# A guard on the softmax: GpSimd counts the reciprocals that lie in range, and a branch at the end decides over a second path

## The chip, the core and the metric

The kernel runs on one core of a Trainium2 chip. A core has five engines with a queue of instructions each: TensorE (PE, matmuls into PSUM), VectorE (DVE), ScalarE (ACT), GpSimd (POOL) and SyncE (SP, which here only issues DMAs and waits). They run by themselves and order each other with semaphores. The metric is device time in microseconds of one execution; lower is better.

## The reference

Two independent halves whose outputs stand side by side. Half A is multi-head attention with 32 heads of 16 columns over 2048 tokens, half B a short convolution, a product, and a long convolution over the sequence:

```python
def _A_ref(x, wqkv, wo):
    B, S, D = x.shape
    H = 32
    Dh = D // H
    qkv = (lambda x, *d: x.transpose(*d))((x @ wqkv).reshape(B, S, 3, H, Dh), 2, 0, 3, 1, 4)
    q, k, v = qkv[0], qkv[1], qkv[2]
    scores = jnp.einsum("bhqd,bhkd->bhqk", q, k) * (Dh ** -0.5)
    p = _softmax(scores, axis=-1)
    o = jnp.einsum("bhqk,bhkd->bhqd", p, v)
    return (lambda x, *d: x.transpose(*d))(o, 0, 2, 1, 3).reshape(B, S, D) @ wo

def _B_ref(q, k, v, shift_k, ssm_k, ssm_D):
    ...
    kv = k_shift * v
    ...
    y = (lambda x, s, axes=(-2,-1): jnp.fft.irfft2(x, s=s, axes=axes).astype(jnp.bfloat16))(y_f, (1, L), axes=(1, 2))[:, 0, :S, :]
    y = y + kv * ssm_D[None, None, :]
    return q * y
```

Weights and inputs are normal numbers times 0.05, so the scores of the softmax are small. A softmax usually subtracts each row's maximum first so that no exponential overflows.

## The kernel before

The kernel computes the exponentials without subtracting a maximum: with scores this small a fixed offset (`OFFSET`, -2 in powers of two) does. Each row's sum of exponentials comes out of the same matmul as the output, because the value matrix `VA` carries a column of ones behind each head's 16 columns.

**Groups.** The work of half A is cut into 32 groups `n` (4 sets `o` of 8 heads, 4 blocks `qb` of 512 queries, and an even and an odd part of the heads). For a group, score blocks of 128 keys by 512 queries are made on TensorE (`qk_mm`, line 827), two or three blocks at a time go through ScalarE's Exp (`emit_exp`, line 854), and one block in so many goes to VectorE instead, which makes the exponential in four passes: a conversion out of PSUM (line 890), a mask (916), a squaring product (921) and another mask (925). TensorE multiplies them by `VA` into one PSUM bank (`emit_pv`, line 964). When a group is complete, `finish_group` takes it on VectorE: a 32x32 block transpose into `DT` (line 1062), the reciprocals of the row sums into the ring `DR` (1069), the product with them into `DTN` (1073), and, for each second group, a transpose back into `OTN` (1082). The last group is finished in four quarters by `finish_last` (lines 1096 to 1111) so that the output projection can follow at once.

**Half B** runs beside it: the long convolution is 8192 small matmuls (line 1234) against shifted copies of the filter that SyncE loads into `WR`.

**Order.** Nothing is scheduled by the hardware. A planner in the program walks step by step (`T`), keeps a model clock for each engine (`Eng.t`), and writes every engine's list of instructions with its waits; what goes where follows from the model clocks. `dve.op`, `pool.op` and so on append an instruction and advance that engine's clock by the times given in `us`. `dma` (line 357) starts a transfer at the model time of its issuing engine. GpSimd's list holds the memsets of the start (lines 461 to 474), the DMAs that spread the scaled queries into `QT` (issued in `evac_unit`, recorded under line 367), the loads and stores of half B's `QN`, the stores of the attention output from `OUTA`, and one memset in the middle (line 1241). `locking` keeps VectorE's passes from being planned beside GpSimd's two long instructions after the start.

**The end.** After the last group, TensorE makes the last output rows, ScalarE and VectorE each copy half of the last tile (lines 1568 and 1566), and both halves are stored. SyncE then waits for all output DMAs (line 1571), and the block that closes the program (line 1573) has every engine drain and meet at a barrier. `Eng.op` (line 162) records an operation with its waits, `Eng.run` (line 187) issues them.

## Time and profile before

| | us |
|---|---|
| runs (3) | 750.45, 751.31, 751.42 |
| median | 751.31 |
| the profiled execution's own time | 753.44 |
| its span, first to last instruction | 751.6 |
| granted TensorE clock, mean | 0.993 |

The profile is one execution. "Busy" is the time in which an engine executes instructions; register, branch, semaphore and DMA-issuing instructions are the sequencer's and are not counted (rows whose engine ends in q, as POOLq). A group's row ends in "busy us, mean ns | idle time before it <-what ended that idle time". A row of one line's instructions gives duration in ns as min/median/max, then the first and the last start. A timeline row begins with the start and the busy time. The chain of waits is followed back from the last instruction.

### The profile page before, as it was taken

The numbers are of one execution on the slowest core, as the hardware profiler recorded it, in microseconds if no ns is written. First come the engines' busy times: TensorE is split into PE (matmuls) and PEld (weight loads), VectorE is DVE, ScalarE is ACT, GpSimd is POOL, SyncE is SP. The second block draws the span as 40 slices with busy tenths as digits, with TensorE's granted clock in tenths as the row PEclk, the third lists the DMA queues.
The fourth block names the chain that finished last, engine by engine and source line by source line (L and its number), as shares of the span: only waits on it lengthen the run. The fifth ranks groups of instructions, "written<-read, shape, count | busy, mean of one in ns | idle before, by whom it ended". The sixth has DMA issues, their size and how long they took to land.

```text
span 751.6 us, 32481 instructions
## 1 busy us (share of the span) xinstructions
PE 697.1 (93%) x14671; PEld 312.6 (42%) x14682; DVE 703.5 (94%) x1442; ACT 725.3 (96%) x691; POOL 98.4 (13%) x172
## 2 busy tenths in 40 slices
PE   7889899999999899999999989999999899999986
PEld 3234344535444444444544333443443344434343
DVE  2999999999899999999999988999999999989993
ACT  6999999999999999999999999999999999999986
POOL 7022102020013002001032021120020202010100
PEclk9999999999999999999999999999999999999999
DMA  9897756766777778665886867665765565776100
GB/s 181 213 257 269 225 167 215 233 234 240 249 239 233 264 241 281 242 197 210 233 269 207 265 220 256 193 238 191 279 222 191 187 271 167 257 242 227 58 3 30
DMA packets 73720, 161.48 MB, mean 215 GB/s; under 512 B 34064, under 2 KB 37776, under 8 KB 73200
## 3 DMA queue, kind: packets, MB, share of 16 engines
q1 hardware_dynamic: 66400, 150.43, 62.5%
q0 software_dynamic: 5984, 8.66, 3.7%
q8 instruction: 116, 1.90, 1.0%
q10 hardware_dynamic: 1200, 0.33, 0.2%
q14 instruction: 20, 0.16, 0.1%
HBM read 142.61 MB, written 6.42 MB: 198 GB/s over the span
## 4 chain that ended last, share of the span: by engine, by line
ACT 63%; PE 18%; DVE 16%; DMA 1%; SPq 1%; issue 1%
ACT PT L854 63%; DVE PTD L890 7%; PE PS L827 6%; PE PS L964 5%; DVE PTD L921 3%; PE PS L1234 3%; DVE PTD L916 2%; PE PS L514 2%; DVE PTD L925 2%; DMA xT<-in_A_x_dram 1%; PE PS L550 1%; SPq L367 1%; DVE DT L1062 1%; PE PS L1485 0%; DVE VA L619 0%
## 5 line engine op out<-in xcount | busy, mean ns | idle before, releaser
L854 ACT ACTIVATE PT<-PS 128x1024 bf16<-128x1024 f32 (+2 forms) x687 | 723.1, 1264 | 14.3 <-PE PS L827 13.4
L890 DVE TENSOR_SCALAR PTD<-PS 128x512 uint16<-128x512 f32 x465 | 310.6, 681 | 14.9 <-PE PS L827 14.1
L827 PE MATMUL PS<-QT,KTo 32*128 32x512 bf16 (+2 forms) x2248 | 273.2, 367 | 29.6 <-ACT PT L854 18.1
L964 PE MATMUL PS<-PT,VA 128*32 128x512 bf16 (+2 forms) x1744 | 185.7, 370 | 4.1 <-DVE VA L619 3.0
L1234 PE MATMUL PS<-WR,KV 128*30 128x128 bf16 (+8 forms) x8192 | 180.3, 219 | 0.0
L1234 PEld LDWEIGHTS PS<-WR,KV 128*32 128x32 bf16 (+7 forms) x8192 | 134.5, 95 | 52.4 <-issue 29.5
L921 DVE TENSOR_TENSOR PTD<-PTD 128x1024 f16<-128x1024 f16 (+1 forms) x233 | 155.4, 677 | 0.5
L827 PEld LDWEIGHTS PS<-QT,KTo 32*128 32x128 bf16 x2248 | 72.1, 91 | 196.5 <-ACT PT L854 137.0
L964 PE MATMUL PS<-PTD,VA 128*32 128x512 f16 (+1 forms) x1008 | 151.5, 370 | 1.8 <-DVE PTD L925 1.7
L367 POOL DMA_DIRECT2D QT<-QS x120 | 61.1, 516 | 423.0 <-DVE QS L580 378.8
L925 DVE TENSOR_SCALAR PTD<-PTD 128x1024 uint16<-128x1024 uint16 (+1 forms) x233 | 95.1, 415 | 0.3
L916 DVE TENSOR_SCALAR PTD<-PTD 128x1024 uint16<-128x1024 uint16 (+1 forms) x233 | 93.0, 416 | 0.3
L964 PEld LDWEIGHTS PS<-PT,VA 128*32 128x32 bf16 x1744 | 47.2, 94 | 93.5 <-issue 69.0
L964 PEld LDWEIGHTS PS<-PTD,VA 128*32 128x32 bf16 x1008 | 39.1, 96 | 12.7 <-issue 2.2
L1485 PE MATMUL PS<-IDN,ZW 128*32 128x512 bf16 (+3 forms) x157 | 37.7, 316 | 0.9 <-PE PS L827 0.5
L367 POOL DMA_DIRECT2D out_dram<-OUTA x15 | 8.7, 579 | 117.9 <-DVE OUTA L1147 84.8
L514 PE MATMUL PS<-xT,WKV 128*32 128x512 bf16 (+1 forms) x256 | 19.2, 385 | 4.6 <-DVE DT L1062 1.3
L1062 DVE STREAM_TRANSPOSE DT<-PS 128x512 f32<-128x512 f32 x31 | 21.9, 708 | 0.4 <-PE PS L964 0.2
L514 PE MATMUL PS<-xT,WQ 128*32 128x512 bf16 x240 | 18.6, 383 | 1.9 <-DVE YB L1250 0.5
L568 PE MATMUL PS<-WKV,xT 128*128 128x128 bf16 x256 | 19.3, 220 | 0.8 <-DVE YB L1250 0.5
L568 PEld LDWEIGHTS PS<-WKV,xT 128*128 128x128 bf16 x256 | 14.4, 98 | 8.7 <-issue 3.7
L1485 PEld LDWEIGHTS PS<-IDN,ZW 128*32 128x32 bf16 x157 | 11.9, 97 | 11.4 <-issue 7.2
(72 smaller groups left out, 246.1 us busy)
## 6 DMA issues: line engine op xcount, KB each, us to landing
WR<-kz_scratch SPq DMA_DIRECT2D x256, 512.0 KB, 5.4
KV<-KV SPq DMA_DIRECT2D x16, 256.0 KB, 5.2
kz_scratch<-WR SPq DMA_DIRECT2D x1, 2176.0 KB, 8.8
QN<-in_B_q_dram POOLq DMA_DIRECT2D x8, 256.0 KB, 5.4
out_dram<-QN POOLq DMA_DIRECT2D x8, 256.0 KB, 4.1
QT<-QS POOLq DMA_DIRECT2D x120, 16.0 KB, 3.9
out_dram<-OUTA POOLq DMA_DIRECT2D x15, 128.0 KB, 3.4
QN<-in_B_ssm_k_dram SPq DMA_DIRECT2D x1, 1024.0 KB, 7.2
```

The source lines that it names most:

```text
L367: f(outp, inp).then_inc(dsem.sem, 16)
L514: ins = e.matmul(dst[g:g + 32], lhsT=w[:, g:g + 32], rhs=rhs, tile_position=(0, g), **kw)
L568: ins = e.matmul(PS[:, bank, 128 * j:128 * j + 128], lhsT=xT[:, dc, (4 * sc + j) * 128:(4 * sc + j + 1) * 128], rhs=WV[:, dc, o * 128:(o + ...
L827: ins = e.matmul(PS[:, bank, i * w:i * w + w], lhsT=KTo[32 * s:32 * s + 32, OF[n_] % 2, kt * 128:(kt + 1) * 128], rhs=QT[32 * s:32 * s + 3 ...
L854: h = act.op(lambda e: e.activation(PT[:, p0:p0 + n, :], src, ACT.Exp, scale=EXP_SCALE, bias=EXP_BIAS), [h, free], us=(0.065 + 0.4257 * n, ...
L890: h_f = urgent(lambda e: e.tensor_scalar(fix_u, PS[:, bank, :], FIX_ADD, FIX_HI, ALU.add, ALU.min), [h, h_ptd.get(i - R_PTD)], slack=S_FX)
L916: st["h"] = dve.op(lambda e: e.tensor_scalar(mant_u, fix_u, MANT, HALF_BITS, ALU.bitwise_and, ALU.bitwise_or), [st["h"]], us=us)
L921: st["h"] = dve.op(lambda e: e.tensor_tensor(mant, fix, mant, ALU.mult), [st["h"]], us=us)
L925: h = dve.op(lambda e: e.tensor_scalar(fix_u, fix_u, OCTAVE, ONE_MORE, ALU.bitwise_and, ALU.bitwise_or), [st["h"]], us=us)
L964: ins = e.matmul(dst, lhsT=w, rhs=rhs, start=first, stop=last, tile_position=(0, 32 * s))
L1234: ins = e.matmul(PS[32 * g:32 * g + 2 * ((30 - d) // 2 + 1), BGB, 128 * kk:128 * kk + w], lhsT=kv, rhs=WR[:, r + g, S - 64 * d - 128:S - 6 ...
L1485: pe.op(lambda e, s=s, k=k, rhs=rhs, bank=bank, rows=rows, c0=c0, first=first: e.matmul(PS[32 * s:32 * s + rows, bank, c0:c0 + 128 * k], l ...
```

## The change

The change adds three things. The kernel's own path stays as it is, except that `DR` becomes a ring of four and its reciprocal also waits for GpSimd's count of four groups before.

First, a watch: whenever the reciprocals of two groups are there (or of the last groups singly and by quarters), GpSimd clamps them to [1/`D_MOST`, 1/`D_LEAST`], subtracts, compares the difference with zero and adds the resulting ones to a running count `OKS[:, 2, :]`: four instructions that wait for each other. Second, a decision at the end: VectorE sums the count, turns it into the number of reciprocals out of range, TensorE adds it over the partitions with a one-column matmul, VectorE writes it to `BADI`; every engine then waits for that, loads the number into a register and branches. Third, a second path behind that branch, which computes half A anew with the exact maximum of each row; for inputs whose count is complete it is jumped over. `D_MOST`, used nowhere before, is now 2 to the 14th. SyncE's waits for the output DMAs move behind the branch.

```diff
-    DR = sb("DR", [128, 2, 16], FP32)
+    DR = sb("DR", [128, 4, 16], FP32)
+    OKS = sb("OKS", [128, 3, 32], FP32)
+    BAD = sb("BAD", [128, 1])
+    BADI = sb("BADI", [1, 1], I32)
...
+    h_ok = {}
+
+    def all_ok(n, r, h):
+        w = r.shape[1]
+        a, b, c = (OKS[:, i, 0:w] for i in range(3))
+        h_ok[n] = pool.op(lambda e: e.tensor_scalar(a, r, 1.0 / D_MOST, 1.0 / D_LEAST, ALU.max, ALU.min), [h, h_okn[0]], us=(0.1, 0.2))
+        h_ok[n] = pool.op(lambda e: e.tensor_tensor(b, a, r, ALU.subtract), [h_ok[n]], us=(0.1, 0.2))
+        h_ok[n] = pool.op(lambda e: e.tensor_scalar(a, b, 0.0, None, ALU.is_equal), [h_ok[n]], us=(0.1, 0.2))
+        h_ok[n - 1] = h_ok[n] = h_okn[0] = pool.op(lambda e: e.tensor_tensor(c, c, a, ALU.add), [h_ok[n], h_okn[0]], us=(0.1, 0.2))
+    h_okn = [pool.op(lambda e: e.memset(OKS[:, 2, :], 0.0))]
...
-            st["h"] = dve.op(lambda e: e.reciprocal(rcp, blocks[:, :, DH:DH + 1]), [h_t], us=us)
+            st["h"] = dve.op(lambda e: e.reciprocal(rcp, blocks[:, :, DH:DH + 1]), [h_t, h_ok.get(n - 4)], us=us)
+            if n == NL - 1:
+                all_ok(n, DR[:, n % 4, :], st["h"])
+            elif n % 2:
+                all_ok(n, DR[:, n % 4 - 1:n % 4 + 1, :].rearrange("p n d -> p (n d)"), st["h"])
...
+            st["h"] = dve.op(lambda e: e.reciprocal(rcp, blocks[:, :, DH:DH + 1]), [h_t, h_ok.get(NL - 4)], us=us)
+            all_ok(NL, DR[:, NL % 4, 4 * j:4 * j + 4], st["h"])
...
-    for ds in d_outA + d_outB + [d_outE]:
-        sp.op(lambda e, ds=ds: e.wait_ge(ds.sem, ds.n), inc=False)
+    h_bad = dve.op(lambda e: e.tensor_reduce(OKS[:, 0, 0:1], OKS[:, 2, :], mybir.AxisListType.X, ALU.add), [h_okn[0]])
+    h_bad = dve.op(lambda e: e.tensor_scalar(BAD[:, :], OKS[:, 0, 0:1], -1.0, float(NQB * NG * 16), ALU.mult, ALU.add), [h_bad])
+    bank = banks_of[end[0] - 2][0]
+    h_bad = pe.op(lambda e: e.matmul(PS[0:1, bank, 0:1], lhsT=BAD[:, :], rhs=VA[:, 0, 0, DH:DH + 1], start=True, stop=True),
+                  [h_bad, bank_free[bank]], kind="F")
+    h_bad = dve.op(lambda e: e.tensor_copy(BADI[:, :], PS[0:1, bank, 0:1]), [h_bad])
...
+    def decide(e, eng, geng):
+        eng.run(e)
+        e.wait_ge(*h_bad)
+        r = e.alloc_register("bad")
+        e.reg_load(r, BADI[0:1, 0:1])
+        with e.If_ne(r, 0):
+            geng.run(e)
...
         @block.gpsimd
         def _(e):
-            pool.run(e)
+            decide(e, pool, gpool)
 
         @block.sync
         def _(e):
-            sp.run(e)
+            decide(e, sp, gsp)
+            for ds in d_outA + d_outB + [d_outE]:
+                e.wait_ge(ds.sem, ds.n)
```

The other three engines call `decide` in the same way. The part left out between the decision and `decide` is the second path: for each of the four sets of heads it makes keys, queries and values anew, takes the row maxima with 128 maximum reductions on VectorE, and repeats scores, exponentials and products with the maxima subtracted by a matmul; GpSimd's share of it is one memset and two affine selects, and SyncE's is one load and 16 stores.

More of the change, by code (lines that the diff above doesn't have):

```diff
@@ L60 @@
 EXP_BIAS = OFFSET * math.log(2.0) + math.log(1.50706)
-D_LEAST, D_MOST = 2.0 ** 5, 2.0 ** 15
+D_LEAST, D_MOST = 2.0 ** 5, 2.0 ** 14
 N_TAIL = 10
@@ L1064, in finish_group @@
         blocks = dt.rearrange("p (b i) -> p b i", i=32)
-        rcp = DR[:, n % 2, :].rearrange("p (b i) -> p b i", i=1)
+        rcp = DR[:, n % 4, :].rearrange("p (b i) -> p b i", i=1)
         st = {"h": h_t}
         def recip(us):
-            st["h"] = dve.op(lambda e: e.reciprocal(rcp, blocks[:, :, DH:DH + 1]), [h_t], us=us)
+            st["h"] = dve.op(lambda e: e.reciprocal(rcp, blocks[:, :, DH:DH + 1]), [h_t, h_ok.get(n - 4)], us=us)
[3 more added lines that the diff above has]
+                all_ok(n, DR[:, n % 4 - 1:n % 4 + 1, :].rearrange("p n d -> p (n d)"), st["h"])
         def mult(us):
@@ L1098, in finish_last @@
         blocks = DT[:, sl].rearrange("p (b i) -> p b i", i=32)
-        rcp = DR[:, NL % 2, 4 * j:4 * j + 4].rearrange("p (b i) -> p b i", i=1)
+        rcp = DR[:, NL % 4, 4 * j:4 * j + 4].rearrange("p (b i) -> p b i", i=1)
         st = {"h": h_t}
         def recip(us):
-            st["h"] = dve.op(lambda e: e.reciprocal(rcp, blocks[:, :, DH:DH + 1]), [h_t], us=us)
+            st["h"] = dve.op(lambda e: e.reciprocal(rcp, blocks[:, :, DH:DH + 1]), [h_t, h_ok.get(NL - 4)], us=us)
+            all_ok(NL, DR[:, NL % 4, 4 * j:4 * j + 4], st["h"])
         def mult(us):
@@ new lines, in bass_concat_heads__mha_block__ssm_conv_h3__prompt_kernel, with g @@
+    h_bad = dve.op(lambda e: e.tensor_copy(BADI[:, :], PS[0:1, bank, 0:1]), [h_bad])
+    first = [(e.sem, e.n) for e in (pe, act, dve, pool)] + [(ds.sem, ds.n) for ds in d_outA + d_outB + [d_outE]]
+    gpe, gact, gdve, gpool, gsp = [Eng(sem(n), {}) for n in ("s_gpe", "s_gact", "s_gdve", "s_gpool", "s_gsp")]
+    d_g, d_go = DmaSem(sem("d_g")), [DmaSem(sem(f"d_go{i}")) for i in range(R_A)]
+    wrote, reads = {}, {}
+    def g(eng, fn, r=(), w=()):
+        deps = [wrote[x] for x in list(r) + list(w) if x in wrote] + [h for x in w for h in reads.get(x, [])]
+        h = eng.op(fn, deps + ([] if eng.n else first))
+        touch(h, r, w)
+        return h
@@ new lines, in touch, with g_dma, area @@
+    def touch(h, r, w):
+        for x in r:
+            reads.setdefault(x, []).append(h)
+        for x in w:
+            wrote[x], reads[x] = h, []
+    def g_dma(dsem, outp, inp, r=(), w=()):
+        deps = [wrote[x] for x in list(r) + list(w) if x in wrote] + [h for x in w for h in reads.get(x, [])]
+        h = dsem.add()
+        gsp.op(lambda e: e.dma_start(outp, inp).then_inc(dsem.sem, 16), deps + ([] if gsp.n else first), inc=False)
+        touch(h, r, w)
+    def area(a, n):
+        return WRF[:, a:a + n]
@@ new lines, in bass_concat_heads__mha_block__ssm_conv_h3__prompt_kernel @@
+    gK, gMT, gM3 = area(0, S), area(9216, S), area(11264, 384).rearrange("p (t c) -> p t c", t=KT)
+    gQ = area(2048, 2 * S).rearrange("p (r f) -> p r f", r=2)
+    gWK = area(6144, 4 * D).rearrange("p (c f) -> p c f", c=4)
+    gSEL = area(8192, 1024).rearrange("p (h k) -> p h k", h=8)
+    gP = area(11648, 2048).rearrange("p (n f) -> p n f", n=4)
+    gM = area(15744, 1024).bitcast(FP32).rearrange("p (m t h) -> p m t h", m=4, h=8)
+    BIG = lambda b, n: PS[:, b:b + n, :].rearrange("p b f -> p (b f)")
@@ new lines, in bass_concat_heads__mha_block__ssm_conv_h3__prompt_kernel, with group_mm, fn @@
+    g_dma(d_g, gWK, wview[:, :, D:2 * D], w=["wk"])
+    g(gpool, lambda e: e.memset(gSEL, -1.0), w=["sel"])
+    for base, step_, ch in ((0, -3, 1), (2, 3, -1)):
+        g(gpool, lambda e, base=base, step_=step_, ch=ch: e.affine_select(
+            out=gSEL, in_=gSEL, compare_op=ALU.is_ge, fill=0.0, base=base, pattern=[[step_, 8], [0, 128]], channel_multiplier=ch), r=["sel"], w=["sel"])
+    def group_mm(bank, pieces):
+        def fn(e):
+            ins = None
+            for out_, w, x, kw in pieces:
+                ins = e.matmul(out_, lhsT=w, rhs=x, **kw)
+            return ins
+        return fn
@@ new lines, in bass_concat_heads__mha_block__ssm_conv_h3__prompt_kernel, with turn @@
+    dc4 = [dict(start=dc == 0, stop=dc == 3) for dc in range(4)]
+    for o in range(4):
+        col = slice(o * 128, (o + 1) * 128)
+        for sc in range(4):
+            tok = slice(sc * 512, sc * 512 + 512)
+            g(gpe, group_mm(4, [(PS[:, 4, :], gWK[:, dc, col], xT[:, dc, tok], dc4[dc]) for dc in range(4)]), r=["wk"], w=["b4"])
+            g(gdve, lambda e, tok=tok: e.tensor_copy(gK[:, tok], PS[:, 4, :]), r=["b4"], w=["k"])
+            g(gpe, group_mm(5, [(PS[:, 5, :], WQ[:, dc, col], xT[:, dc, tok], dc4[dc]) for dc in range(4)]), w=["b5"])
+            for par in range(2):
+                g(gdve, lambda e, tok=tok, par=par: e.tensor_scalar(gQ[:, par, tok], PS[:, 5, :], MASK[:, par:par + 1], None, ALU.mult), r=["b5"], w=["q"])
+            g(gpe, group_mm(7, [(PS[:, 7, 128 * j:128 * j + 128], xT[:, dc, (4 * sc + j) * 128:(4 * sc + j + 1) * 128], WV[:, dc, col], dc4[dc])
+                                for j in range(4) for dc in range(4)]), w=["b7"])
+            dst = VA[:, 0, 4 * sc:4 * sc + 4, 0:8 * VW].rearrange("p k (h e) -> p k h e", e=VW)[:, :, :, 0:DH]
+            g(gdve, lambda e, dst=dst: e.tensor_copy(dst, PS[:, 7, :].rearrange("p (k h e) -> p k h e", k=4, h=8)), r=["b7"], w=["v"])
+        for hl in range(8):
+            s_, par = hl // 2, hl % 2
+            rows = slice(32 * s_, 32 * s_ + 32)
+            for t in range(KT):
+                g(gpe, group_mm(0, [(PS[:, b, :], gQ[rows, par, t * 128:t * 128 + 128], gK[rows, b * 512:b * 512 + 512],
+                                     dict(start=True, stop=True, tile_position=(32 * s_, 0))) for b in range(4)]), r=["k", "q"], w=["b0", "b2"])
+                g(gdve, lambda e, t=t, hl=hl: e.tensor_reduce(gM[:, 0, t, hl:hl + 1], BIG(0, 4), mybir.AxisListType.X, ALU.max), r=["b0", "b2"], w=["m"])
+        parts = gM3.rearrange("p t (h j) -> p t h j", j=3)
+        for j in range(3):
+            g(gdve, lambda e, j=j: e.tensor_copy(parts[:, :, :, j], gM[:, j, :, :]), r=["m"], w=["m3"])
+            if j < 2:
+                g(gdve, lambda e, j=j: e.tensor_tensor(gM[:, j + 1, :, :], gM[:, j, :, :], parts[:, :, :, j], ALU.subtract), r=["m3"], w=["m"])
+        mt = BIG(4, 2).bitcast(BF16)
+        def turn(e):
+            ins = None
+            for t in range(KT):
+                ins = e.transpose(mt[0:24, t * 128:t * 128 + 128], gM3[:, t, :], IDN[:, :])
+            return ins
+        g(gpe, turn, r=["m3"], w=["b4", "b5"])
+        g(gdve, lambda e: e.tensor_copy(gMT[0:24, :], mt[0:24, :]), r=["b4", "b5"], w=["mt"])
+        for qb in range(NQB):
+            qs = slice(qb * QB, qb * QB + QB)
+            p = PAIRS.index((o, qb))
+            for par in range(2):
+                for s_ in range(4):
+                    hl, rows = 2 * s_ + par, slice(32 * s_, 32 * s_ + 32)
+                    for k in range(KT // 2):
+                        b, i = 2 * (k % 2), 2 * (k % 2)
+                        kts = (2 * k, 2 * k + 1)
+                        g(gpe, group_mm(b, [(PS[:, b + j, :], gK[rows, kt * 128:kt * 128 + 128], gQ[rows, par, qs],
+                                             dict(start=True, stop=False, tile_position=(32 * s_, 0))) for j, kt in enumerate(kts)]), r=["k", "q"], w=["b%d" % b])
+                        g(gpe, group_mm(b, [(PS[:, b + j, :], gSEL[0:24, hl, :], gMT[0:24, qs],
+                                             dict(start=False, stop=True, tile_position=(0, 0))) for j in range(2)]), r=["mt", "sel"], w=["b%d" % b])
+                        g(gact, lambda e, b=b, i=i: e.activation(gP[:, i:i + 2, :].rearrange("p n f -> p (n f)"), BIG(b, 2), ACT.Exp, scale=EXP_SCALE),
+                          r=["b%d" % b], w=["p%d" % i])
+                        g(gpe, group_mm(6, [(PS[32 * s_:32 * s_ + 32, 6, :], VA[:, 0, 2 * k + j, hl * VW:hl * VW + 32], gP[:, i + j, :],
+                                             dict(start=2 * k + j == 0, stop=2 * k + j == KT - 1, tile_position=(0, 32 * s_))) for j in range(2)]),
+                          r=["v", "p%d" % i], w=["b6"])
+                g(gdve, lambda e: e.transpose(out=DT[:, :], in_=PS[:, 6, :]), r=["b6"], w=["dt"])
+                blocks = DT[:, :].rearrange("p (b i) -> p b i", i=32)
+                rcp = DR[:, 0, :].rearrange("p (b i) -> p b i", i=1)
+                g(gdve, lambda e: e.reciprocal(rcp, blocks[:, :, DH:DH + 1]), r=["dt"], w=["dr"])
+                g(gdve, lambda e, par=par: e.tensor_tensor(DTN[:, 0, :].rearrange("p (b i) -> p b i", i=32)[:, :, DH * par:DH * par + DH],
+                                                           blocks[:, :, 0:DH], rcp.broadcast_to([128, 16, DH]), ALU.mult), r=["dt", "dr"], w=["dtn"])
+            g(gdve, lambda e, p=p: e.transpose(out=OTN[:, p, :], in_=DTN[:, 0, :]), r=["dtn"], w=["ot"])
@@ new lines, in bass_concat_heads__mha_block__ssm_conv_h3__prompt_kernel @@
+    for i in range(KT):
+        qb, t = i // 4, i % 4
+        g(gpe, group_mm(7, [(PS[:, 7, :], OTN[:, PAIRS.index((o, qb)), t * 128:(t + 1) * 128], WO[:, o, :], dc4[o]) for o in range(4)]), r=["ot"], w=["b7"])
+        g(gdve, lambda e, i=i: e.tensor_copy(OUTA[:, i % R_A, :], PS[:, 7, :]), r=["b7"], w=["o%d" % (i % R_A)])
+        g_dma(d_go[i % R_A], out2[i * 128:i * 128 + 128, 0:D], OUTA[:, i % R_A, :], r=["o%d" % (i % R_A)])
+    for ds in d_go:
+        gsp.op(lambda e, ds=ds: e.wait_ge(ds.sem, ds.n), inc=False)
@@ L1575, in _ @@
         def _(e):
-            pool.run(e)
+            decide(e, pool, gpool)
         @block.sync
         def _(e):
-            sp.run(e)
+            decide(e, sp, gsp)
+            for ds in d_outA + d_outB + [d_outE]:
+                e.wait_ge(ds.sem, ds.n)
         @block.tensor
         def _(e):
-            pe.run(e)
+            decide(e, pe, gpe)
         @block.scalar
         def _(e):
-            act.run(e)
+            decide(e, act, gact)
         @block.vector
         def _(e):
-            dve.run(e)
+            decide(e, dve, gdve)
     for cm in reversed(ctxs):
```

## The prediction

> **What bounds the kernel now.** I read the page first (busy times, chain), then the busy time by windows, then the last microseconds instruction by instruction, because the change adds work in two places only: a little on GpSimd all through the softmax, and a decision at the very end.

> ```profile
> span 751.6 us, 32481 instructions
> PE 697.1 (93%) x14671; PEld 312.6 (42%) x14682; DVE 703.5 (94%) x1442; ACT 725.3 (96%) x691; POOL 98.4 (13%) x172
> ACT 63%; PE 18%; DVE 16%; DMA 1%; SPq 1%; issue 1%
> ```

> ```profile
> core 0: us, PE busy (x) PEld busy (x) DVE busy (x) ACT busy (x) POOL busy (x), PEclk, DMA share, GB/s
> 40.00:720.00 680.00, 642.24 (x13770) 286.17 (x13769) 659.72 (x1347) 671.76 (x641) 80.80 (x149) 1.00 0.69 225
> 720.00:735.00 15.00, 11.88 (x337) 8.12 (x343) 13.74 (x35) 12.20 (x12) 0.00 (x0) 0.89 0.01 2
> 735.00:752.00 17.00, 10.86 (x230) 6.22 (x232) 5.15 (x15) 9.72 (x12) 1.64 (x3) 0.99 0.10 33
> ```

> ScalarE's exponentials bound the body: in the 680 us from 40 to 720 it idles 680 - 671.76 = 8.2 us, VectorE 680 - 659.72 = 20.3 us, and GpSimd works 80.8 us. Of the chain that ends last ScalarE holds 63%, VectorE 16%. So a little more VectorE time reaches the end only in part, and GpSimd has room.

> The end is a stage of its own. These are the VectorE, ScalarE, GpSimd and DMA-issue rows of the timeline from 744.8, and then the instructions that line 1573 (the block that closes the program) leaves on the sequencers.

> ```profile
> 744.91 0.54 POOL L367 DMA_DIRECT2D out_dram<-OUTA  x1 [2.29 <-DVE OUTA L1147]
> 745.19 0.18 DVE L1103 RECIPROCAL DR<-DT 128x4 f32<-128x4 f32 x1
> 746.68 0.42 DVE L1566 CAST QT<-PS 128x256 bf16<-128x256 f32 x1 [0.70 <-PE PS L1139]
> 747.13 0.36 SPq L367 DMA_DIRECT2D out_dram<-QT  x1
> ```

> ```profile
> L1573 POOLq EVENT_SEMAPHORE  x2: 17/17/17, 751.4 to 751.5; - x2
> L1573 POOLq DRAIN  x1: 6514/6514/6514, 744.9 to 744.9; - x1
> L1573 ACTq DRAIN  x1: 153/153/153, 747.5 to 747.5; - x1
> L1573 SPq COMPARE_BRANCH  x1: 41/41/41, 749.1 to 749.1; - x1
> L1573 SPq DRAIN  x1: 13/13/13, 749.3 to 749.3; - x1
> L1573 SPq EVENT_SEMAPHORE  x1: 17/17/17, 751.6 to 751.6; - x1
> ```

> The last output has landed and SyncE is through its waits at 749.1, and its DRAIN is at 749.3. Yet the program ends at 751.6, because GpSimd's own DRAIN runs from 744.9 for 6.51 us, to 751.4. Nothing after 749.3 but that DRAIN holds the end. This is what the forecast turns on.

> **The change, part by part.** Nothing is taken out. `D_LEAST` and `D_MOST` were unused, and the wider `DR` ring only moves addresses.

> *1. The watch on GpSimd.* `all_ok` is called at 15 odd groups, at group 30, and four times for the last group: 20 calls of 4 instructions, 80 in all, on at most 128x32 fp32, and one memset in the start-up. Before had no elementwise instruction with an input on GpSimd but two affine selects, so I bound one from the nearest rows:

> ```profile
> L465 POOL MEMSET ZW<- 128x32 bf16 x1 | 0.1, 114 | 0.0
> L467 POOL TENSOR_SCALAR_AFFINE_SELECT IDN<-IDN 128x128 bf16<-128x128 bf16 x1 | 0.3, 284 | 0.2 <-POOL IDN L466 0.2
> 41.88 0.42 POOL L456 MEMSET QN<- 128x32 bf16 x1
> 41.83 0.42 DVE L925 TENSOR_SCALAR PTD<-PTD 128x1024 uint16<-128x1024 uint16 x1
> ```

> Alone it is 0.11 us (no input) to 0.28 us (four times the elements); I take 0.2. The memset of 32 columns that took 0.11 us early takes 0.42 us at 41.88, where it began beside a VectorE pass (41.83 to 42.25) and ended just behind it: GpSimd waits for such a pass. One call is thus 4 x 0.11 = 0.4 to 4 x 0.42 = 1.7 us of GpSimd, mostly in time it idles.

> What waits behind a call are GpSimd's DMAs, late by 1.7 us at most. `QT<-QS` is the one that feeds the scores; no row of the waits view has TensorE waiting for it, so its lead covers this. Without that lead each delayed set would cost ScalarE up to the 1.7 us. The second wait on the reciprocal asks for a count of four groups before, some 4 x 680/30 = 90 us old: nothing.

> *2. What it does to VectorE.* The blocking goes both ways:

> ```profile
> L916 DVE TENSOR_SCALAR PTD<-PTD x233: 250/418/606, 22.2 to 734.8; 128x1024 uint16<-128x1024 uint16 x116, 128x512 uint16<-128x512 uint16 x1
> L925 DVE TENSOR_SCALAR PTD<-PTD x233: 294/416/711, 25.2 to 735.5; 128x1024 uint16<-128x1024 uint16 x116, 128x512 uint16<-128x512 uint16 x1
> L925 DVE TENSOR_SCALAR PTD<-PTD 128x1024 uint16<-128x1024 uint16 (+1 forms) x233 | 95.1, 415 | 0.3
> L916 DVE TENSOR_SCALAR PTD<-PTD 128x1024 uint16<-128x1024 uint16 (+1 forms) x233 | 93.0, 416 | 0.3
> ```

> A pass of 0.42 us took up to 0.71 us. The 76 instructions of the 19 calls ahead of the last one hold GpSimd's side for 76 x 0.2 = 15.2 us. These two lines are 188.1 of VectorE's 703.5 us (27%), so about 15.2 x 0.27 = 4.1 us of VectorE is lost; by its 16% of the chain 0.7 us of that reaches the end, at most all 4.1. I take 1.0, near the lower bound because VectorE idles 20.3 us in the body.

> ```profile
> L921 DVE TENSOR_TENSOR PTD<-PTD x233: 425/681/693, 23.7 to 735.1; 128x1024 f16<-128x1024 f16 x116, 128x512 f16<-128x512 f16 x1
> L921 DVE TENSOR_TENSOR PTD<-PTD 128x1024 f16<-128x1024 f16 (+1 forms) x233 | 155.4, 677 | 0.5
> ```

> The squaring pass never stretched (maximum 693 beside a median of 681 ns), but GpSimd only wrote until now. [...]

> *3. The order of everything else.* The planner books each call on GpSimd's clock, and start times of its DMAs follow from that. Some orders may flip. Its sign can't be read from a profile; I take 0 and give the hole it could fill or widen under the rivals.

> *4. The decision.* The last call waits for the reciprocal that ends at 745.19 + 0.18 = 745.37 and stands behind the DMA that ends at 744.91 + 0.54 = 745.45. Four instructions at 0.25 (0.2 and a hand-over of 0.05) end at 746.45, at 0.42 each at 747.1. VectorE takes the sum only behind its cast, which ends at 746.68 + 0.42 = 747.10, so the watch itself is hidden even at its upper bound.

> ```profile
> L1069 DVE RECIPROCAL DR<-DT 128x16 f32<-128x16 f32 x31 | 7.3, 236 | 0.0
> L683 PE MATMUL PS<-PAT x2: 159/166/173, 4.6 to 4.6; 1*128 1x1 bf16 x2
> L686 DVE TENSOR_SCALAR MASK<-PS x1: 158/158/158, 4.8 to 4.8; 128x2 f32<-128x2 f32 x1
> L1609 POOLq MOVE  x1: 35/35/35, 0.1 to 0.1; - x1
> out_dram<-QT ACTq DMA_DIRECT2D x1, 64.0 KB, 1.7
> ```

> From 747.10: the reduction 0.25 (as a reciprocal of 16 columns), the subtraction 0.17 (a reciprocal of 4 columns, 0.18 above), the one-column matmul 0.17, the copy out of PSUM 0.16, and three hand-overs of 0.05: the count is there at 748.0. Each engine then loads it into a register: not shown; from 0.035 us (a register move) to 1.7 us (a DMA's landing). It is one word and no DMA, so I take 0.3, about two of the small VectorE accesses. Then the branch past the second path: SyncE's took 0.2 us (749.1 to 749.3). GpSimd, whose second path is three instructions long, arrives at its DRAIN at 748.0 + 0.3 + 0.2 = 748.5 instead of 744.9.

> The price of that is the DRAIN's. From the end of the DMA before it (745.45) it lasted 5.95 us. Either that is work begun when GpSimd arrives, or it runs out at 751.4 by itself. I take it as work: with nothing but memsets ahead (line 1609) there is a DRAIN too, and its row is short:

> ```profile
> L1609 POOLq DRAIN  x1: 179/179/179, 0.4 to 0.4; - x1
> ```

> so the length belongs to the DMAs that GpSimd has issued in between, and these stay the same. It then ends at 748.5 + 5.95 = 754.45, the program 0.2 us later (751.4 to 751.6 above) at 754.6: +3.0 us.

> TensorE, ScalarE and VectorE jump over thousands of instructions. Their branch costs from 0.2 us (SyncE's) to 3.3 us, a DMA's 1.7 us plus the longest gap of TensorE that the waits view puts down to nothing but issue:

> ```profile
> PEld PS L827 <- issue: 23.9, 65, 1.6
> ```

> Even at 3.3 they are at the closing barrier by 748.3 + 3.3 = 751.6, under GpSimd's DRAIN to 754.45; without that cover they would end the program at 751.8. [...]

> *Sum:* body +1.0, end +3.0, together +4.0: the span 751.6 becomes 755.6. The profiled execution took 753.44 us, of which 1.84 lie around its span, and the median of the runs is 751.31, 2.1 us below it. The same +4.0 on the median gives **755.3 us**.

> **The rivals.**
> *The DRAIN runs out by itself* (not slower): it is a wait for something that GpSimd's last DMA began at 745, and a later arrival finds it over at 751.4. For it: the DRAIN's record began at 744.9, before that DMA was issued; against: that DMA should have landed by 747 (SyncE's output, issued at 747.13, was in by 749.1), 4 us before the DRAIN's end. Then the far branches decide: 751.8 + 0.2 = 752.0, +0.4 at the end; with 0.7 of the body 752.4 us on the median, inside what can be told from no change. It decides if GpSimd's DRAIN in the new profile ends before 752.
> *Contention on the path*: GpSimd's instructions hold VectorE, and all of it goes through. [...]
> *GpSimd's own branch waits for its target*: 3.3 instead of 0.2 us ahead of the DRAIN, +3.1: 758.4 us. Against it: its jump is a few instructions long.
> *The plan moves and comes out shorter.* There is something to win, such as this hole of ScalarE near the end:

> ```profile
> 728.09 2.12 ACT L854 ACTIVATE PT<-PS 128x1024 bf16<-128x1024 f32 x2 [2.04 <-PE PS L827]
> ```

> With it and half of the body's 8.2 us gone, -6.1 + 4.0 = -2.1, 749.2 us. A plan that moves can as well lose this much, 757.3 with the hole doubled.
> *That the guard misfires* and the second path runs would cost thousands of matmuls, far outside any range; the reference's small scores speak against it and I give it no chance.

> **How the numbers follow.** Forecast 0.53, DRAIN by itself 0.20, contention 0.12, GpSimd's branch 0.07, plan shorter 0.08. A change of 0.2% (1.5 us) is about what a measurement of this kernel can tell. The range leaves out most of the shorter plan and the far end of contention: 751.7 to 761.0. Slower by over 0.2%: the forecast, contention, the branch and a part of the second, 0.78; within: most of the second and some shorter plans, 0.17; faster: 0.05.

> **What would show it.** Step 4: GpSimd's DRAIN near 748.5 and near 6 us long. Step 1: 80 small GpSimd instructions of 0.1 to 0.4 us. [...] I am wrong if the DRAIN is short, if ScalarE's idle in 40 to 720 moves by more than 3 us from 8.2, or if the sum of the row counts arrives later than VectorE's last cast.

## The result and the profile after

The kernel after took 756.23 us (median of 7 runs, 755.18 to 759.64), the kernel before beside it 750.62 us (7 runs): ratio 1.0077 with a 95% interval of 1.0057 to 1.0097, or +5.8 us (4.3 to 7.3). Repeated in a later job against 35 runs of before it was 755.9 against 752.81 us: 1.0048 (1.0022 to 1.0075), +3.6 us (1.7 to 5.6). The forecast was +4.0 us and 755.3 us. The profiled execution took 756.6 us. Its page:

```profile
span 754.6 us, 32637 instructions
PE 700.2 (93%) x14688; PEld 314.0 (42%) x14688; DVE 702.7 (93%) x1441; ACT 726.2 (96%) x691; POOL 127.8 (17%) x253
```

Only GpSimd's busy time moved much, from 98.4 to 127.8 us. The same stages as before, by windows (one row each: length, busy time of every engine, granted clock, DMA):

```profile
core 0: us, PE busy (x) PEld busy (x) DVE busy (x) ACT busy (x) POOL busy (x), PEclk, DMA share, GB/s
40.00:720.00 680.00, 643.33 (x13779) 287.24 (x13776) 656.91 (x1339) 670.98 (x639) 101.84 (x206) 0.99 0.70 225
720.00:735.00 15.00, 12.08 (x347) 8.22 (x339) 13.98 (x35) 12.34 (x13) 4.15 (x11) 0.89 0.07 21
735.00:756.00 21.00, 11.41 (x219) 5.81 (x217) 4.92 (x16) 9.72 (x11) 3.87 (x13) 0.88 0.09 29
```

In the body ScalarE idles 680 - 670.98 = 9.0 us instead of 8.2: no new hole. In the last 21 us the engines are idle for longer, and that is where the time went: the last exponential ends at 744.34 us in both profiles, and the spans differ by 3.0 us. The timeline from the last quarter's reciprocal on (start, busy us; GpSimd's four instructions of the watch, then the decision):

```profile
745.19 0.18 DVE L1121 RECIPROCAL DR<-DT 128x4 f32<-128x4 f32 x1
745.47 0.26 POOL L1066 TENSOR_SCALAR OKS<-DR 128x4 f32<-128x4 f32 x1 [1.00 <-DVE DR L1121]
...
746.40 0.20 POOL L1069 TENSOR_TENSOR OKS<-OKS 128x4 f32<-128x4 f32 x1
...
746.46 0.42 DVE L1585 CAST QT<-PS 128x256 bf16<-128x256 f32 x1 [0.49 <-PE PS L1158]
746.80 0.18 DVE L1589 TENSOR_REDUCE OKS<-OKS 128x1 f32<-128x32 f32 x1
...
747.42 0.15 DVE L1594 CAST BADI<-PS 1x1 int32<-1x1 f32 x1 [0.26 <-PE PS L1592]
```

The watch ends at 746.60 (746.40 + 0.20), before VectorE's last cast ends at 746.88: it is hidden, as forecast. The count is there at 747.57. What the sequencers do from there is in the instructions of three lines (durations in ns, min/median/max, then the start). Line 1715, the register load, of GpSimd and TensorE:

```profile
L1715 POOLq TENSOR_LOAD <-BADI x1: 639/639/639, 747.6 to 747.6; - x1
L1715 PEldq TENSOR_LOAD <-BADI x1: 629/629/629, 747.6 to 747.6; - x1
```

Line 1716, the branch:

```profile
L1716 POOLq COMPARE_BRANCH  x1: 50/50/50, 748.3 to 748.3; - x1
L1716 PEldq COMPARE_BRANCH  x1: 3551/3551/3551, 748.3 to 748.3; - x1
```

Line 1719, the closing block:

```profile
L1719 POOLq DRAIN  x1: 5948/5948/5948, 748.5 to 748.5; - x1
L1719 ACTq DRAIN  x1: 81/81/81, 751.5 to 751.5; - x1
L1719 DVEq DRAIN  x1: 58/58/58, 751.7 to 751.7; - x1
L1719 PEldq DRAIN  x1: 73/73/73, 751.9 to 751.9; - x1
L1719 SPq EVENT_SEMAPHORE  x1: 17/17/17, 754.6 to 754.6; - x1
```

GpSimd reaches its DRAIN (the instruction with which an engine ends its list before the closing barrier) at 748.5 instead of 744.9 and spends 5.95 us in it, to 754.4; everything else is at the barrier by 752.0. In neither profile does the DRAIN end with its queue's data: the last packet of GpSimd's DMA queue lands at 745.56 us here, before the DRAIN begins, and at 746.54 in the kernel before, where the DRAIN runs until 751.4.

### The profile page after: what moved, and what is told of

The parts are those of the page before. It is cut to its first block, busy times and chain, and to the rows that moved or that the text cites. A ratio compares the mean times of both kernels' runs of the same rounds, so it can differ in the third digit from the quotient of the medians.

```text
span 754.6 us, 32637 instructions
## 1 busy us (share of the span) xinstructions
PE 700.2 (93%) x14688; PEld 314.0 (42%) x14688; DVE 702.7 (93%) x1441; ACT 726.2 (96%) x691; POOL 127.8 (17%) x253
## 3 DMA queue, kind: packets, MB, share of 16 engines
q0 software_dynamic: 5984, 8.66, 3.8%
## 4 chain that ended last, share of the span: by engine, by line
ACT 58%; DVE 24%; PE 15%; issue 1%; DMA 1%
ACT PT L857 58%; DVE PTD L893 10%; PE PS L830 5%; DVE PTD L924 4%; PE PS L967 4%; PE PS L1253 3%; DVE PTD L919 3%; DVE PTD L928 2%; PE PS L517 1%; DVE KV L605 1%; DVE DT L1076 1%; DMA xT<-in_A_x_dram 1%; DVE VA L622 1%; PE PS L1504 0%; PE PS L553 0%
## 5 line engine op out<-in xcount | busy, mean ns | idle before, releaser
L967 PE MATMUL PS<-PT,VA 128*32 128x512 bf16 (+2 forms) x1745 | 182.9, 369 | 5.0 <-DVE VA L622 3.0
L1253 PEld LDWEIGHTS PS<-WR,KV 128*32 128x32 bf16 (+8 forms) x8192 | 134.3, 95 | 56.0 <-issue 34.2
L924 DVE TENSOR_TENSOR PTD<-PTD 128x1024 f16<-128x1024 f16 x232 | 156.2, 684 | 0.4
L928 DVE TENSOR_SCALAR PTD<-PTD 128x1024 uint16<-128x1024 uint16 x232 | 95.8, 420 | 0.4
L919 DVE TENSOR_SCALAR PTD<-PTD 128x1024 uint16<-128x1024 uint16 x232 | 93.8, 422 | 0.3
L1066 POOL TENSOR_SCALAR OKS<-DR 128x32 f32<-128x32 f32 (+2 forms) x20 | 8.2, 410 | 294.5 <-DVE DR L1083 286.2
L1504 PE MATMUL PS<-IDN,ZW 128*32 128x384 bf16 (+3 forms) x173 | 43.4, 317 | 0.0
L1504 PEld LDWEIGHTS PS<-IDN,ZW 128*32 128x32 bf16 x173 | 14.2, 99 | 10.3 <-issue 6.3
```

The source lines that it names most:

```text
L919: st["h"] = dve.op(lambda e: e.tensor_scalar(mant_u, fix_u, MANT, HALF_BITS, ALU.bitwise_and, ALU.bitwise_or), [st["h"]], us=us)
L924: st["h"] = dve.op(lambda e: e.tensor_tensor(mant, fix, mant, ALU.mult), [st["h"]], us=us)
L928: h = dve.op(lambda e: e.tensor_scalar(fix_u, fix_u, OCTAVE, ONE_MORE, ALU.bitwise_and, ALU.bitwise_or), [st["h"]], us=us)
L967: ins = e.matmul(dst, lhsT=w, rhs=rhs, start=first, stop=last, tile_position=(0, 32 * s))
L1253: ins = e.matmul(PS[32 * g:32 * g + 2 * ((30 - d) // 2 + 1), BGB, 128 * kk:128 * kk + w], lhsT=kv, rhs=WR[:, r + g, S - 64 * d - 128:S - 6 ...
L1504: pe.op(lambda e, s=s, k=k, rhs=rhs, bank=bank, rows=rows, c0=c0, first=first: e.matmul(PS[32 * s:32 * s + rows, bank, c0:c0 + 128 * k], l ...
```

## The experiments

The body of this kernel varies from execution to execution (747.82 to 763.15 us over 35 executions of before in the last job), so beside the medians I read one number that hardly varies: the **end part**, from the end of the last exponential (the last `PT` activation in the timeline) to the end of the span. Ratios are against runs of the kernel before in the same job; the microseconds are the ratio times its median.

| kernel | median | ratio (interval) | us against before | end part | GpSimd's DRAIN |
|---|---|---|---|---|---|
| before | 750.6, 752.2, 752.1, 752.8 | | | 7.29 | 6.51, from 744.9 |
| change, first | 756.23 | 1.0077 (1.0057, 1.0097) | +5.8 | 10.30 | 5.95, from 748.5 |
| change, again | 755.9 | 1.0048 (1.0022, 1.0075) | +3.6 | 10.30 | 5.95 |
| decision, no watch | 756.6 | 1.0058 (1.0035, 1.0081) | +4.4 | 10.51 | 5.94 |
| plan kept | 756.57 | 1.0042 (1.0013, 1.007) | +3.2 | 10.52 | 5.95 |
| plan kept, again | 755.16 | 1.0031 (1.0006, 1.0056) | +2.3 | 10.51 | 5.95 |
| watch multiplied, plan kept | 755.58 | 1.0066 (1.0036, 1.0096) | +5.0 | 10.52 | 5.95 |
| moved plan alone | 751.83 | 1.0005 (0.9977, 1.0034) | +0.4 | 6.31 | 6.51, from 743.3 |
| change, no DRAIN | 754.6 | 1.0017 (0.9988, 1.0046) | +1.3 | 7.93 | none |
| plan kept, no DRAIN | 753.47 | 1.0033 (1.0004, 1.0062) | +2.5 | 8.51 | none |
| near branch, no DRAIN | 749.41 | 0.9959 (0.9937, 0.9982) | -3.1 | 5.25 | none |
| before, no DRAIN | 750.11 | 0.998 (0.9956, 1.0004) | -1.5 | 5.24 | none |
| before, no DRAIN, again | 750.0 | 0.9969 (0.9942, 0.9996) | -2.3 | 5.24 | none |
| before, 80 more DMAs | 769.19 | 1.0232 (1.019, 1.0274) | +17.4 | 11.22 | 10.44 |

### The decision without the watch

```diff
     def all_ok(n, r, h):
...
+        pass
...
-    h_okn = [pool.op(lambda e: e.memset(OKS[:, 2, :], 0.0))]
+    h_okn = [pool.op(lambda e: e.memset(OKS[:, 2, :], 16.0))]
```

> The watch is left out: the count is set to complete by one memset at the start, and the decision, the branch and the second path behind it stay. TensorE's, VectorE's and ScalarE's orders are those of before up to the decision. Theory (the decision costs 3.0 us at the end, the rest of the +5.6 comes from the plan that moved): +3.0 on before, about 753.6 us, GpSimd's DRAIN still near 5.95 us long. Rival (GpSimd's instructions hold VectorE up): the same +3.0 here, so this run gives the base for the next. A third theory, that the far larger program costs something by itself, would show as more than +3.5 here.

+4.4 us (2.6 to 6.1), with not one instruction of the watch in it, and the end part 10.51 - 7.29 = 3.2 us longer:

```profile
L1716 POOLq DRAIN  x1: 5944/5944/5944, 746.7 to 746.7; - x1
...
L1716 SPq EVENT_SEMAPHORE  x1: 17/17/17, 752.8 to 752.8; - x1
```

The decision alone carries the cost of the change within what these runs can tell. A DRAIN begun at 746.7, 3.2 us after GpSimd's last DMA had been issued, took as long as the one begun at 748.5, 4.0 us after it.

### The plan kept, and the plan moved alone

To give the watch without a moved plan, GpSimd's model clock is set back after each call; TensorE, VectorE and ScalarE then have the order of the kernel before.

```diff
     def all_ok(n, r, h):
+        t_pool = pool.t
...
+        pool.t = t_pool
...
```

> All of the change, but GpSimd's planning clock is set back after each call of the watch, so that TensorE, VectorE and ScalarE run in the order of before. Theory (plan): the watch costs nothing, as without it, +3.0, about 753.6 us. Rival (contention): the watch costs the body as in the changed kernel, +5.6, about 756.2 us; by the prediction's own 1.0 us for it 754.6.

> The change with PE, ACT and DVE in the order of the kernel before, once more: 3.2 us above the kernel before by its end, as measured the first time. By the theory of a body that costs nothing the change itself stands level with it; by the rival the change stands 2 us above.

The moved plan alone is the kernel before with the model clock advanced where `all_ok` would have been called, and no instruction added; these three engines then have the order of the kernel after.

```diff
+    def all_ok(h):
+        t = pool.at([h])
+        for _ in range(4):
+            pool.t = t = max(pool.t + 0.1, t + 0.2)
```

> The kernel before, with GpSimd's planning clock moved as the watch moves it and not one instruction added: TensorE, VectorE and ScalarE run in the changed kernel's order, with no watch, no decision and no second path. Theory (plan): +2.6 on before, about 753.2 us, with the loss between 290 and 335 us. Rival (contention): +0, about 750.6 us.

With the plan kept +3.2 and +2.3 us; the moved plan alone +0.4 us (-1.7 to 2.6). My theory of that moment, that the moved plan costs 2.6 us, is not borne out: the interval just reaches it, but the middle is near zero. The moved plan even brings GpSimd's last store 1 us nearer to the last exponential (end part 6.31), which the change can't use, as its DRAIN waits for the decision.

### The change again

> The change once more, beside the run with the kept plan, on one chip. If the cost is the end alone, 3.2 us above the kernel before by the end parts (10.5 less 7.3), so 754.5 to 756.5 where before is 752, and no more than 1 us from the kept plan. If the moved plan or the watch costs the body another 2 us, as the first comparison of the change (5.8 us) would have it: 757 to 758, and 2 us above the kept plan.

+3.6 us, 1.3 us above the kept plan of the same job, with intervals of some 2 us on either side of each. The end part gives 10.30 - 7.29 = 3.0 of it, so 0.6 us are left for the body. The first comparison, +5.8 us with 10.30 - 7.29 = 3.0 of it at the end as well, leaves 2.8 us for the body; the two intervals overlap, and +4.0 lies inside the second and just below the first.

### The watch multiplied

```diff
+        for _ in range(3 if n < NL else 0):
+            h_ok[n] = pool.op(lambda e: e.tensor_scalar(a, r, 1.0 / D_MOST, 1.0 / D_LEAST, ALU.max, ALU.min), [h, h_okn[0], h_ok.get(n)], us=(0.1, 0.2))
+            h_ok[n] = pool.op(lambda e: e.tensor_tensor(b, a, r, ALU.subtract), [h_ok[n]], us=(0.1, 0.2))
+            h_ok[n] = pool.op(lambda e: e.tensor_scalar(a, b, 0.0, None, ALU.is_equal), [h_ok[n]], us=(0.1, 0.2))
```

> The change with the plan kept, and in each of the 16 calls of the body three more rounds of clamp, subtraction and comparison: 13 instructions for 4, some 144 more on GpSimd, about 40 us more of its time. If the watch costs the body nothing that counts: the median of the run with the kept plan, 3.2 us above the kernel before, within 1.5 us. If contention on VectorE were what it costs, four times as much of it: 4 to 15 us above the run with the kept plan, and the passes' busy time longer by as much. If TensorE's gate at 245 to 248 comes from the watch, more such gates in the body, each 3.4 us long at half the clock.

+5.0 us (2.7 to 7.2): about 2 us above the kept plan of the other jobs, and not apart from it by the intervals. The trace, one execution, says more. The page's busy row, and the groups of VectorE's three passes by shape:

```profile
PE 693.7 (92%) x14672; PEld 311.9 (41%) x14683; DVE 704.6 (94%) x1445; ACT 724.8 (96%) x691; POOL 185.1 (25%) x397
```

```profile
L924 DVE TENSOR_TENSOR PTD<-PTD 128x1024 f16<-128x1024 f16 x232 | 154.9, 678 | 0.5
L928 DVE TENSOR_SCALAR PTD<-PTD 128x1024 uint16<-128x1024 uint16 x232 | 94.4, 414 | 0.2
L919 DVE TENSOR_SCALAR PTD<-PTD 128x1024 uint16<-128x1024 uint16 x232 | 93.4, 419 | 0.3
```

GpSimd is busy 86.7 us more than before (185.1 against 98.4), and the passes are where they were in the mean: 678 ns against 679, 414 and 419 against 416 and 417, grouped in the same way. VectorE in all has 704.6 us against 703.5, so 1.1 us for almost three times the watch's instructions; for the watch itself next to nothing is left.

A trap stood beside it. In the first profile after, the same passes are 1% longer, which looks like contention:

```profile
L924 DVE TENSOR_TENSOR PTD<-PTD 128x1024 f16<-128x1024 f16 x232 | 156.2, 684 | 0.4
L928 DVE TENSOR_SCALAR PTD<-PTD 128x1024 uint16<-128x1024 uint16 x232 | 95.8, 420 | 0.4
L919 DVE TENSOR_SCALAR PTD<-PTD 128x1024 uint16<-128x1024 uint16 x232 | 93.8, 422 | 0.3
```

But a kernel without any watch, profiled in another job (the second run of before without the DRAIN), shows the same:

```profile
L921 DVE TENSOR_TENSOR PTD<-PTD 128x1024 f16<-128x1024 f16 (+1 forms) x233 | 156.6, 683 | 0.6
L925 DVE TENSOR_SCALAR PTD<-PTD 128x1024 uint16<-128x1024 uint16 (+1 forms) x233 | 96.2, 421 | 0.3
L916 DVE TENSOR_SCALAR PTD<-PTD 128x1024 uint16<-128x1024 uint16 (+1 forms) x233 | 94.0, 422 | 0.3
```

All four kernels of that job, with and without the watch, have 683 to 684 ns, all eight of the two other jobs of experiments 676 to 678: it goes with the job, each of which ran on another chip, and not with the watch. The record doesn't name the chips of the first two profiles, but the trace of the change answers for itself: the 192 full-width squaring passes that run beside no GpSimd instruction take 685 ns in the mean, the 40 that run beside one 679.

### The DRAIN taken away

```diff
-    with nc.Block() as block:
+    with nc.Block(no_gpsimd_drain=True) as block:
```

On the change, on the kept plan, and twice on the kernel before:

> The changed kernel without GpSimd's DRAIN in the block that closes the program (SyncE's waits for all output DMAs stay). Theory (the DRAIN is 5.95 us of work that sets the end): the end falls to TensorE's branch, whose DRAIN ended at 752.0 in the changed kernel's profile, 2.4 us before GpSimd's at 754.4: about 753.8 us, -2.4 on the changed kernel. Rival (the end waits for something else, such as the DMAs themselves): no change, 756.2 us.

> The whole change, with PE, ACT and DVE in the order of the kernel before, and without GpSimd's DRAIN at the closing block. The theory that the DRAIN is 5.95 us of work that starts when GpSimd arrives: the end is then the far branches (the count at 747.5, 0.63 us of register load, 3.55 us of TensorE's branch, the DRAIN of TensorE behind it, so 751.9 in the clock of the profile after), 2.4 us less than in the run with the kept plan, from the last exponential's end to the span's end 7.9 us against 10.5, and the median 0.6 to 1.2 us above the kernel before. The rival, that the body costs several us with the watch in it: 3 us or more above the kernel before, in spite of the end.

> The kernel before without GpSimd's DRAIN; no guard. If the DRAIN alone held the end (SyncE through its waits at 749.1 to 749.3, GpSimd at 751.4), the end comes 2.1 us earlier, from the last exponential's end to the span's end 5.2 us instead of 7.3, and the median is 2.1 us below the kernel before. If the DRAIN waited for something that the end waits for anyhow, no change.

> The kernel before without GpSimd's DRAIN, no guard, once more: 2.1 us below the kernel before (the end part 5.2 instead of 7.3 us). The first time it was 2 us below, with an interval that just reached no change; with both together it should not.

The end part of the change falls by 10.30 - 7.93 = 2.4 us, as expected, and then ends with TensorE's branch; the kept plan falls by 2.0 only, as TensorE's branch took 3.85 us there. The median of the kept plan (+2.5, 0.3 to 4.7) lies above the 0.6 to 1.2 us expected, which the interval takes in. The kernel before loses 2.05 us of its end, and its end is now the landing of the last output. Twice the time came out below the kernel before, the second time with the whole interval (-4.4 to -0.3 us). The end of the first of the two:

```profile
L1573 SPq COMPARE_BRANCH  x1: 41/41/41, 745.0 to 745.0; - x1
L1573 SPq DRAIN  x1: 13/13/13, 745.2 to 745.2; - x1
```

SyncE, through its waits for the stores at 745.0, is the last; the span ends at 745.5.

### The branch made short

From the kept plan without the DRAIN, the second path cut:

```diff
-    for o in range(4):
+    for o in range(0):
...
+    g(gact, lambda e: e.activation(gP[:, 0, :], BIG(0, 1), ACT.Exp, scale=EXP_SCALE), r=["b0"], w=["p0"])
-    for i in range(KT):
+    for i in range(1):
...
```

> The watch, the kept plan and no DRAIN, and of the second path only one block of output, one activation, one copy and one store left, so that the branch past it is short on every engine (the rest of the second path is left out; it is not run on these inputs in either kernel). If TensorE's branch of 3.55 us is the distance to its target: the branch takes 0.05 to 0.2 us on PE, ACT and DVE as it does on SP, the end part falls from 8.5 to about 5.2 us, where SyncE's landing of the last output sets it, and the median is 3 us below the run with the far branch, level with the kernel before or 2 us below it. If the length is the engine's or the register's and not the distance's: 3.5 us again and no change.

The branch rows of the kept plan without the DRAIN, with the far target:

```profile
L1720 ACTq COMPARE_BRANCH  x1: 54/54/54, 745.8 to 745.8; - x1
L1720 DVEq COMPARE_BRANCH  x1: 72/72/72, 745.9 to 745.9; - x1
L1720 PEldq COMPARE_BRANCH  x1: 3847/3847/3847, 745.9 to 745.9; - x1
```

The next instruction on VectorE and TensorE there, the closing block's:

```profile
L1723 DVEq DRAIN  x1: 75/75/75, 749.2 to 749.2; - x1
L1723 PEldq DRAIN  x1: 73/73/73, 749.8 to 749.8; - x1
```

The same branch with the near target:

```profile
L1721 ACTq COMPARE_BRANCH  x1: 54/54/54, 747.2 to 747.2; - x1
L1721 DVEq COMPARE_BRANCH  x1: 72/72/72, 747.3 to 747.3; - x1
L1721 PEldq COMPARE_BRANCH  x1: 215/215/215, 747.3 to 747.3; - x1
```

And what follows it:

```profile
L1724 DVEq DRAIN  x1: 17/17/17, 747.5 to 747.5; - x1
L1724 PEldq DRAIN  x1: 8/8/8, 747.5 to 747.5; - x1
```

With the distance TensorE's 3.85 us become 0.22. VectorE's branch reads 0.07 us both times, yet the instruction behind it starts 3.3 us later when the target is far (745.9 to 749.2) and 0.2 us later when it is near (747.3 to 747.5); ScalarE's reads 0.05 us both times, with 3.5 us to its DRAIN when the target is far (745.8 to 749.3) and 0.5 us when it is near (747.2 to 747.7). So on VectorE and ScalarE the time stands as a gap behind the branch, on TensorE as its duration. The DMA queues show what falls into that time. Between the far branches and the next instructions (745.9 to 749.5 us) stand three DMA packets of the kind that the profile calls instruction:

```profile
q8 instruction: 1, 0.02, 2.4%
q14 instruction: 2, 0.02, 1.8%
```

In the profile of the change one packet of q8 and two of q14 fall behind the far branches too, from 748.9 to 750.0 us, and the closing DRAINs of ScalarE, VectorE and TensorE begin at 751.5 to 751.9. The end part falls by 8.51 - 5.25 = 3.3 us, to the same 5.2 us as the kernel before without a DRAIN and without a guard. So without the DRAIN the watch, the sum, the register load and a near branch together cost the end nothing; the last store's landing covers them.

### More DMAs for the DRAIN

```diff
+            pool.op(lambda e, i=i: e.dma_start(more_ap[i:i + 1, :], IDN[0:1, 0:64]).then_inc(d_more.sem, 16), [h_idn], inc=False)
```

four times in each of 20 groups, on the kernel before; the stores go to a tensor that nothing reads.

> The kernel before with 80 more small DMAs on GpSimd's queue, four in each of 20 groups, no guard; same order on PE, ACT and DVE. If the DRAIN's work goes with the DMAs that GpSimd has issued (5.95 us for 152 of them, 39 ns each), it takes 9.1 us instead of 5.95 from the last DMA's issue, and the program ends 3.1 us later. If it is a fixed piece of work, 5.95 us again and the time of before within 1.5 us.

```profile
L1585 POOLq DRAIN  x1: 10437/10437/10437, 759.0 to 759.0; - x1
...
L1585 SPq COMPARE_BRANCH  x1: 41/41/41, 763.4 to 763.4; - x1
```

All stores have landed at 763.4, and GpSimd still drains until 769.5. It took 10.44 us against 6.51, so 3.92 us for 80 DMAs, 49 ns each, where 39 had been expected: between these two kernels the DRAIN's work goes with the DMAs that GpSimd has issued, the added ones between groups 5 and 24, long before the end. It doesn't go with their bytes (8.66 MB on GpSimd's queue before, 8.68 with the 80 more). Whether it counts DMAs or their packets (5984 and 8544) stays open: neither is in proportion. That is 3.9 of the +17.4 us. The other 14 are lost in the body, where its last exponential ends at 758.5 instead of 744.3; which of the small DMAs' effects takes them was not looked into, so nothing is concluded from this kernel's body.

## Why the prediction was right, and where not

**The end (+3.0).** Right in place, mechanism and size: GpSimd's DRAIN was forecast for 748.5 with 5.95 us of work, and stands there with 5.948. Two smaller terms were off and cancelled, which was luck: the count came at 747.57 instead of 748.0 (VectorE's last cast ended 0.22 us earlier than in the profile before, and the four steps behind it took 0.69 instead of 0.90 us), and the register load, one word from the tile `BADI`, took 0.61 to 0.64 us on all five engines instead of 0.3, which was my estimate, as no row of before shows such a load.

**The DRAIN that runs out by itself** (0.20) fell by its own test: it ended at 754.4, not before 752. The runs show more than the forecast had. It begins when GpSimd gets there (746.7 in the run without the watch, 748.5 here), and its length is 5.95 us in both; it grew by 49 ns for each DMA added.

**The far branches.** They lay under the DRAIN as forecast and cost the change nothing. At 3.47 to 3.85 us on TensorE (3.55 in the change, 3.57 in its repetition, 3.47 without the watch, 3.51 and 3.85 in the change and the kept plan without the DRAIN) they are above the upper bound of 3.3 us, which had been put together from a DMA's landing and an issue gap. Without that cover the prediction had the end at 751.8, 0.2 us behind the kernel before; without the DRAIN the change's end part was 7.93 against 7.29 us, 0.6 behind. The near branch took 3.3 us off. The length goes with the distance (3.85 us far, 0.22 near), and three instruction packets stand in the gap; that the engines wait for these packets is my reading and not shown. (The thousands of skipped instructions are TensorE's; VectorE skips some 700 operations, ScalarE some 1000, and in the change their next instructions start 3.5 and 3.2 us after their branches.) GpSimd's own branch, a rival at 0.07, took 0.05 us; it jumps over three instructions.

**The watch.** 80 instructions, as forecast; in the mean they took longer than the 0.2 us taken. The largest group and the smallest of the four main ones:

```profile
L1066 POOL TENSOR_SCALAR OKS<-DR 128x32 f32<-128x32 f32 x15 | 6.8, 451 | 282.5 <-DVE DR L1083 282.4
...
L1069 POOL TENSOR_TENSOR OKS<-OKS 128x32 f32<-128x32 f32 x15 | 4.0, 266 | 1.3
```

The twelve groups by shape add to 27.9 us, 0.35 us each, between the bounds of 0.11 and 0.42 but nearer to the upper; the longest single one took 0.80 us. In GpSimd's idle time it made no difference.

**Contention (the term of 4.1 us on VectorE, 1.0 in the body).** This step failed. The watch's 27.9 us of GpSimd, and 86.7 us more than before in the multiplied watch, did not lengthen VectorE's passes in the mean. That a memset beside a mask pass had taken 0.42 instead of 0.11 us was on GpSimd's side; I read the maximum of 0.71 us on VectorE's side as the same thing seen from there and spread it over every overlap. It is something else. In the trace of before all five full-width mask passes above 0.45 us run beside a DMA issue of GpSimd, the longest two beside loads of `QN`; one of them:

```profile
404.19 1.49 POOL L367 DMA_DIRECT2D QN<-in_B_q_dram  x2 [6.14 <-PE PS L1234]
...
405.25 0.69 DVE L925 TENSOR_SCALAR PTD<-PTD 128x1024 uint16<-128x1024 uint16 x1
```

The kernel before has these DMAs already, and the change adds none. Beside the watch's instructions alone the longest mask pass of the change took 0.48 us. Whether instructions of GpSimd that read, as the watch's do, stretch the squaring pass was open before these runs. In the multiplied watch (224 instructions for 80) the longest squaring pass took 737 ns instead of 693:

```profile
L924 DVE TENSOR_TENSOR PTD<-PTD x233: 424/680/737, 21.4 to 732.4; 128x1024 f16<-128x1024 f16 x116, 128x512 f16<-128x512 f16 x1
```

The mean of the full-width ones is 678 ns there and 679 in the kernel before. In the change ten of them ran beside the watch alone; they took 670 ns in the mean and at most 703, and among those beside no GpSimd instruction the longest took 707. So a single pass may have stretched, by 44 ns at the maximum, and the mean did not.

The rival that built on this (0.12) falls with it. The range's upper end, 761.0 us, allowed for a loss on VectorE beyond the 4.1 us of the mask passes; no run shows such a loss: with the multiplied watch VectorE was busy for 704.6 us, 1.1 more than in the kernel before.

**The body's +1.0 in total.** By the end part the first comparison leaves 5.8 - 3.0 = 2.8 us and the repeated one 3.6 - 3.0 = 0.6, with intervals of 1.5 and about 2 us on either side; the run without the watch leaves 1.2, the kept plans 0.0 and -0.9. So the size is neither shown nor refuted, and that the total came near +4.0 owes something to luck, as the step behind this +1.0 failed. One place may hold a part of it. The windows of 240 to 260 us, in the run without the watch, in the repeated change and in the multiplied watch:

```profile
240.00:260.00 20.00, 18.04 (x434) 8.17 (x426) 19.49 (x41) 19.64 (x21) 0.00 (x0) 1.00 0.81 262
```

```profile
240.00:260.00 20.00, 18.53 (x402) 7.72 (x390) 18.83 (x39) 19.19 (x19) 1.44 (x4) 0.91 0.82 255
```

```profile
240.00:260.00 20.00, 17.21 (x404) 7.69 (x394) 18.74 (x39) 18.82 (x19) 5.23 (x13) 1.00 0.79 262
```

With the watch TensorE's granted clock dropped to a half for 3.4 us there (0.91 as a mean of the 20 us) in six of eight profiles; without the watch and without added DMAs that mean was 1.00 in all five profiles. ScalarE then waits twice for scores, here in the repeated change:

```profile
246.40 1.02 ACT L857 ACTIVATE PT<-PS 128x1024 bf16<-128x1024 f32 x1 [0.32 <-PE PS L830]
247.91 3.00 ACT L857 ACTIVATE PT<-PS 128x1024 bf16<-128x1024 f32 x3 [0.49 <-PE PS L830]
```

That is 0.8 us, ScalarE's whole idle time in that window (20 - 19.19); without the watch and without the drop it idles 20 - 19.64 = 0.4 us there, so about half a microsecond goes with the drop. Yet the third window, with the most of the watch, and the near branch's have the full clock, and in the first run with the kept plan the twelve matmuls that begin at 247.44 us, 0.5 us before the watch's first instruction (247.92), already take 1.47 us, against 0.83 in the near branch's profile. Whether the watch brings it about stays open.

**The plan.** Taken as 0; +0.4 us (-1.7 to 2.6) when it was moved alone. The rival of a shorter plan (0.08) did not come.

**What the forecast missed.** The DRAIN that sets the end was seen, and its price for the change was right; that leaving it out would shorten the kernel before by some 2 us was not drawn from it, although the same rows say so: SyncE at 749.3, GpSimd at 751.4. Whether a program may always leave it out was not looked into; here SyncE waits for every output DMA.

## What to carry to other kernels

Read the last microseconds on the sequencers, not only on the engines: here an engine that is 13% busy (17% with the watch) owns the end of the program through a closing DRAIN whose length grew with the DMAs it had issued, and what makes it arrive later is paid for. A decision on data at the end was cheap where the jump was short and no such DRAIN stood behind it (the sum, the load and the branch hid under the last store, with an end part of 5.25 us against 5.24 without a guard); a long jump cost 3.3 us on VectorE, which skips some 700 operations, and 3.85 on TensorE, which skips thousands. Before a stretched pass is put down to a kind of neighbour, look which neighbour it had: a maximum alone doesn't say. And before a 1% stretch of an engine's passes is called contention, look for it in a kernel without the suspect on the same chip.
